# An attention and mixture-of-experts kernel: leftover router weights on VectorE, earlier router steps, and work queued behind the third tile

## Chip, cores and metric

One core of a Trainium2 chip. The metric is device time in microseconds (us) of one execution. The engines are named as in the profile: PE is TensorE, with its weight loads apart as PEld; DVE is VectorE, ACT ScalarE, POOL GpSimd, SP SyncE, which issues most of the transfers.

## What is computed

```python
# q, k, v: (8, 8, 576, 64); causal window of 128, a bias by distance, softmax
attn_out = _attn_ref(**attn_kwargs)
x = attn_out.transpose(0, 2, 1, 3).reshape(B * S, H * D)      # 4608 tokens x 512
logits = x @ w_gate                                           # 8 experts
for idx in np.argsort(-logits.flatten()):                     # best pairs first
    tok, e = idx // E, idx % E
    if assigned[tok] >= 0 or counts[e] >= cap: continue       # cap = 576
    assigned[tok] = e; counts[e] += 1
for e in range(E):
    mask = assigned == e
    out[mask] = np.maximum(x[mask] @ w1[e], 0) @ w2[e]        # 512 -> 1024 -> 512
```

Each expert gets exactly 576 tokens. The assignment is greedy over all token-expert pairs, so the experts fill one after the other.

## The kernel before

**Attention** works on 32 pairs of heads in a software pipeline, with an order written out by hand, and takes the first 204 us or so. It leaves the token rows x in DRAM and the router's scores `L_sb` on the chip.

**The router** (`Router`) finds the experts in the order in which they fill: phase k yields the list of the 576 tokens (`idx[k]`) and the number (`ei[k]`) of the k-th expert to fill. A phase is a chain of small VectorE operations and tiny matmuls on PE that count tokens over 64 thresholds at a time. Phases are Python generators: each `yield` ends a step, and the code that lays out the expert matmuls calls `next(route)` at chosen places, so that the steps lie between matmuls. Phase 0 is `phase0`, driven through `go()` inside `first_expert`; phases 1 to 7 are `phase`. A phase begins with `first_choice` (each token's best expert among the weights that are left: b, ne, cand, am, OH), goes on with `ends`, three counting rounds in `few` (a step ending in an indicator `ind`, a step with the count matmuls and `sat`, and so on), then `totals`, `members`, `positions`, `hits` and `rows`, which writes `idx`. `later` (L908 to L920) then works out the weights left over for the next phase, `L1`; after it come four small operations on a flag that asks for an exact second pass if something did not come out.

**The experts** (`MoE`). The tokens of an expert are gathered by GpSimd in five tiles g of 128 rows (the last of 64), `gather`. `flip` transposes a tile with four PE transposes into the PSUM tile pg (one buffer) and ScalarE copies it rounded into xh; `under` has VectorE write the remainder xl = pg - xh. Weights come in four chunks of 512 KB for each layer (`raw`, four buffers); `split` makes `hl` from each: ScalarE casts the high part (L1041), VectorE subtracts two halves of the low part (L1047, `low`). A layer then takes three matmuls for each product (high x high, low x high, high x low). Layer 1 sums into ph (four buffers), ScalarE applies the relu into hh (L1116), VectorE writes the remainder hlo (L1127). Layer 2 sums into po; its result o is scattered by GpSimd (L1167).

The second expert's layer 1 runs in halves (tokens 0 to 287 first, then the rest), so it can begin when three of its five tiles are turned.

**The order of work.** While `r.nc` and `m.nc` are `OrderedCore`, each engine keeps the order in which the program names its instructions; their records all show L463, the helper's line. After `r.nc = m.nc = nc` the scheduler of the framework orders the instructions by priority (their order in the program) and modelled readiness. GpSimd and SP are never held by `OrderedCore`.

- In `first_expert`, `go(n)` takes n steps of phase 0, `m.low` a weight half on VectorE, `keep_warm(n)` issues n matmuls on zeros (numbers in `ZEROS`).
- Layer 2 of the first expert is laid out with a stop after each of its 40 groups of matmuls (eight for each of five tiles; three matmuls in a group, two in the last tile's). `ROUTE_2`, `ROUTE_3`, `LOAD_2`, `SPLIT_2` and `TURN_2` name the groups behind which a step of the router, a load of a weight chunk of the second expert, a `split` of a chunk, or a flip of one of its tiles is put. What is left of the splits and flips follows behind group 40, with the unordered engines.
- From the second expert on, `slot(k, i)` runs at 31 places i of expert k (0 to 15 in layer 1, 16 to 30 in layer 2). It takes a router step if the waiting count allows and phase k + 1 is not done, or phase k + 2 is not done and i has reached `AHEAD[min(k, 2)]`; it loads and splits by `W_LOAD` and `W_SPLIT`; from i = 16 on it gathers and flips the next expert's tiles.

Of the kernel before, what the change touches and what calls it, by code (L numbers as in the profile page):

```python
# [418 lines left out]

CONST_AT = 4  # L420
WARM, WARM0, WARM1 = 11, 16, 4
AHEAD = 18, 0, 0
ZEROS = 2, 4, 1, 2, 5
CHOICE_1 = 1, 4
HIGHS_2 = 0, 3, 4, 5
LOWS_2 = 0, 0, 0, 2, 1, 2, 2, 1
ROUTE_2 = 11, 12, 14, 15, 17, 18, 19, 22, 26
ROUTE_3, SOONER = (33, 37), (1, 2)
LOAD_2 = {20: 2, 33: 1, 37: 1}
SPLIT_2 = 31, 33  # L430
TURN_2 = 36, 38, 40
W_LOAD = [(0, 1, 0, 0), (0, 1, 1, 2), (0, 1, 2, 6), (0, 1, 3, 10),
          (1, 0, 0, 13), (1, 0, 1, 16), (1, 0, 2, 19), (1, 0, 3, 22), (1, 1, 0, 28)]
W_SPLIT = [(0, 1, 0, 2), (0, 1, 1, 6), (0, 1, 2, 10), (0, 1, 3, 14),
# [36 lines left out]
class Router:  # L471
# [287 lines left out]
    def phase0(self):  # L759

        nc, rt, rs = self.nc, self.p["rt"], self.p["rs"]
        self.pen = self.small("pen", 8)
        nc.vector.memset(self.pen, 0.0)
        nc.vector.tensor_copy(self.left, self.C["e8"])
        b, am, OH = self.b0, self.am0, self.OH0
        lo, w, rw = self.first
        c0, cl = FIRST - 1, self.c0
        self.clamp(cl, b, lo, w, c0)
        key = self.place(cl, lo, rw, c0)
        ind = rt.tile([128, NT, J], BF, name="ind", bufs=1)  # L770
        for a, z in self.halves(c0, NT):
            self.indicate(ind, key, a, z)
        cnt = self.count(ind, OH, c0, NT)
        w2, low = self.small("w"), self.small("low")
        nc.vector.tensor_tensor(low, lo, w, ALU.subtract)
        nc.vector.tensor_scalar(w2, w, 1.0 / J, None, ALU.mult)
        self.place(cl, lo, rw, 0, c0, key)
        rw2 = self.small("rw")
        nc.vector.tensor_scalar(rw2, rw, float(J), None, ALU.mult)
        lo, m, ex, v = self.first_full(cnt, self.part, key, am, w, low)  # L780
        w, rw = w2, rw2
        key = self.place(cl, lo, rw)
        hits = self.ahead_hits(m, ex)
        for s in (1, 2):
            ind = rt.tile([128, NT, J], BF, name="ind", bufs=1)
            for i, (a, z) in enumerate(self.halves(0, NT)):
                if s == 1 and i == 0:
                    self.indicate(ind, key, a, z)
                    self.ahead_rows(hits)
                    yield  # L790
                else:
                    self.indicate(ind, key, a, z)
            low = self.small("low")
            nc.vector.tensor_tensor(low, lo, w, ALU.subtract)
            if s == 1:
                w2, rw2 = self.small("w"), self.small("rw")
                nc.vector.tensor_scalar(w2, w, 1.0 / J, None, ALU.mult)
                nc.vector.tensor_scalar(rw2, rw, float(J), None, ALU.mult)
            yield
            cnt = self.count(ind, OH, 0, NT)  # L800
            yield
            n = self.enough(cnt, self.pen)
            next(n)
            yield
            try:
                next(n)
            except StopIteration as e:
                n = e.value
            yield
            if s == 1:  # L810
                lo2 = self.small("lo")
                nc.vector.scalar_tensor_tensor(lo2, w, n[:, 0:1], low, ALU.mult, ALU.add)
                lo, w, rw = lo2, w2, rw2
                key = self.place(cl, lo, rw)
        sel, rest = (rt.tile([128, NT], BF, name=name, bufs=1) for name in ("sel0", "rsel"))
        nc.vector.tensor_scalar(sel, key[:, :, 0], 1.0, n[:, 0:1], ALU.add, ALU.is_ge)
        nc.vector.tensor_tensor(rest, self.rest, sel, ALU.mult)
        m, ex = self.members(am, v[:, 0:1], rest, NT)
        nc.vector.scalar_tensor_tensor(self.hi, w, n[:, 0:1], low, ALU.mult, ALU.add)
        sp = self.bank()  # L820
        self.positions(sp, m, ex, NT)
        nc.tensor.matmul(sp[:, 64:65], self.C["ones"], self.run[:, NT - 1:NT], start=True, stop=True)
        yield
        hits = self.hits(sp, m, NT, 3, nc.scalar, 2)
        off = self.small("off")
        nc.vector.tensor_scalar(off, sp[:, 64:65], float(CAP - AHEAD_ROWS), None, ALU.not_equal)
        yield
        idx = rs.tile([128, 5], I32, name="idx", bufs=4)
        self.rows(self.bank(), hits, NT, 3, idx)
        self.idx[0] = [self.few_rows[:, t:t + 1] for t in range(2)] + [idx[:, t:t + 1] for t in range(3)]  # L830
        yield
        T1 = rt.tile([128, 8, NT], BF, name="T1")
        nc.vector.tensor_tensor(T1, OH, bc(sel.unsqueeze(1), [128, 8, NT]), ALU.mult)
        nc.vector.tensor_tensor(self.flag, self.flag, off, ALU.max)
        yield
        Dc, keyv, mx = self.totals(T1)
        yield
        nc.vector.tensor_tensor(off, mx, v, ALU.not_equal)
        nc.vector.tensor_tensor(self.flag, self.flag, off, ALU.max)
        self.later(0, self.L0, T1, Dc, keyv, mx)  # L840
        yield

    def halves(self, c0, c1):
# [16 lines left out]
    def phase(self, k, exact=False):  # L860
# [38 lines left out]
        self.later(k, L, T1, Dc, keyv, mx)  # L899
        if k == 1:  # L900
            yield 0

    def later(self, k, L, T1, Dc, keyv, mx):

        nc, rt = self.nc, self.p["rt"]
        if k < 7:
            self.pen = self.small("pen", 8)
            nc.vector.tensor_scalar(self.pen, Dc, float(CAP), -BIG, ALU.is_ge, ALU.mult)  # L908
            self.base = self.small("base", 8)
            nc.vector.tensor_tensor(self.base, self.pen, Dc, ALU.add)  # L910
            nc.vector.scalar_tensor_tensor(self.left, keyv, mx[:, 0:1], self.left, ALU.not_equal, ALU.mult)
            L2 = rt.tile([128, 8, NT], F32, name="L2", bufs=1)
            eng = nc.vector if k == 0 else self.tc.nc.gpsimd
            eng.tensor_tensor(L2, L, bc(self.pen.unsqueeze(2), [128, 8, NT]), ALU.add)
            if k == 0:
                nc.vector.scalar_tensor_tensor(self.L1, T1, 100.0 * BIG, L2, ALU.mult, ALU.add)
            else:
                Lt = rt.tile([128, 8, NT], F32, name="Lt", bufs=1)
                eng.tensor_scalar(Lt, T1, 100.0 * BIG, 1.0, ALU.mult, ALU.mult)
                eng.tensor_tensor(self.L1, Lt, L2, ALU.add)  # L920
        ov = self.small("ov")
        nc.vector.tensor_reduce(ov, Dc, AX.X, ALU.max)
        nc.vector.tensor_scalar(ov, ov, float(CAP), None, ALU.is_gt)
        nc.vector.scalar_tensor_tensor(ov, mx, 0.0, ov, ALU.is_equal, ALU.max)
        nc.vector.tensor_tensor(self.flag, self.flag, ov, ALU.max)
# [98 lines left out]
class MoE:  # L1024
# [61 lines left out]
    def under(self, h, r, ps):  # L1086

        xh, xl = (x[:, :, 128 * h:128 * h + r] for x in self.xg)
        self.nc.vector.tensor_tensor(xl, ps[:, :, :r], xh.bitcast(F32), ALU.subtract)  # L1089

    def turn(self, gs):

        for h, g, r in gs:
            self.under(*self.flip(h, g, r))
            yield

    def hidden(self):

# [119 lines left out]
def first_expert(tc, P, C, r, m, route):  # L1218
# [7 lines left out]
    def go(n=1):  # L1226
        for _ in range(n):
            next(p)
# [24 lines left out]
    m.idle = P["ps_h"].tile([128, 512], F32, name="ph")  # L1253
    W = [m.high(raw[c]) for c in range(2)]
    go(2)
    m.low(W[0], raw[0], 0)
    m.keep_warm(ZEROS[0])
    go(2)
    m.low(W[0], raw[0], 1)
    m.keep_warm(ZEROS[1])  # L1260
    go(2)
    m.low(W[1], raw[1], 0)
    a0 = m.flip(*ga[0], "o")
    m.keep_warm(ZEROS[2])
    go(2)
    a1 = m.flip(*ga[1])
    m.keep_warm(ZEROS[3])
    go()
# [55 lines left out]
            m.low(*lows.pop(0))  # L1324
    rest(7, 1)
    next(route)
    return V


def layer_moe(tc, P, C, r, m, exact):  # L1330
# [12 lines left out]
    def part(e, layer):  # L1343
        W[e, layer].append(m.split(raws[e, layer][len(W[e, layer])]))
# [25 lines left out]
    if exact:  # L1370
        r.start(True)
        W[0, 0] = [m.split(raw) for raw in m.loads(r.ei[0], 0)]
        for _ in m.turn(m.gather(r.idx[0])):
            pass
        for _ in m.layer1(W.pop((0, 0))):
            pass
        V = [m.split(raw) for raw in m.loads(r.ei[0], 1)]
        while 1 not in r.idx:
            next(route)
    else:  # L1380
        V = first_expert(tc, P, C, r, m, route)
    i = 0
    for _ in m.layer2(V, m.h, r.idx[0], fine=True):
        i += 1
        if i in ROUTE_2 and not exact:
            next(route)
        if i == ROUTE_2[-1]:
            r.nc = nc
            gathers[0] = m.turn(m.gather(r.idx[1]))
        if i in ROUTE_3:  # L1390
            next(route)
        for _ in range(LOAD_2.get(i, 0)):
            load(1, 0)
        if i in SPLIT_2:
            part(1, 0)
        if i in TURN_2:
            next(gathers[0])
    r.nc = m.nc = nc
    while len(W[1, 0]) < 4:
        part(1, 0)  # L1400
    for _ in gathers[0]:
        pass
    for k in range(1, E):
        i = 0
        for _ in m.layer1(W.pop((k, 0)), k == 1):
# [95 lines left out]
```

## Time and profile before

| | |
|---|---|
| median of 3 runs | 697.83 us (696.14 to 698.83) |
| the profiled execution: its own time | 698.43 us |
| its span, first to last instruction | 696.7 us |
| mean granted PE clock | 0.979 |
| PE busy | 664.7 us (95%) |
| VectorE busy | 459.6 us (66%) |
| ScalarE busy | 326.7 us (47%) |
| GpSimd busy | 150.5 us (22%) |
| first expert's first matmul | 223.69 us |
| second expert's first matmul | 291.07 us |

A row of a timeline reads: start in us, duration in us, engine, line, operation, out<-in, count, and in brackets the time that the engine stood idle before it and what ended that. A row of sums by stretch reads: stretch, its length, then the busy time and the number of instructions of PE, PEld, VectorE, ScalarE and GpSimd, the mean PE clock, the busy share of the DMA engines and GB/s.

### The profile page before, as it was taken

What the parts mean: (1) busy time and instruction counts of PE and PEld (TensorE: products, weight loads), DVE (VectorE), ACT (ScalarE), POOL (GpSimd) and SP (SyncE); (2) the same over time, 40 slices, a digit from 0 to 9 for tenths busy, and PEclk for the clock granted to TensorE, in tenths of its full rate; (3) what the DMA queues carried; (4) which work ended last, traced back from release to release, by engine and by line L of the source; (5) the groups of instructions that cost most, each with busy time, mean ns of one, the idle gap of its engine ahead of it and who ended that gap; (6) DMA issues with size and microseconds to landing.
All of it is one profiled execution on the core that took longest, in us unless ns stands there. A gap on an engine that the chain in (4) does not pass through costs nothing.

```text
span 696.7 us, 18902 instructions
## 1 busy us (share of the span) xinstructions
PE 664.7 (95%) x7274; PEld 582.6 (84%) x7274; DVE 459.6 (66%) x1903; ACT 326.7 (47%) x992; POOL 150.5 (22%) x337
## 2 busy tenths in 40 slices
PE   8999999999967999799999999999999999999995
PEld 5899899988864987598689789889988988988985
DVE  6778887887878777789698738828847525423310
ACT  6998898988942431523243233224314324322210
POOL 4122222122211103303231231131132022011011
PEclk9999999999995999799999999999999999999999
DMA  8475766667324504604546245145135325201001
GB/s 300 150 229 178 222 196 208 202 205 210 108 70 144 168 16 151 211 1 171 185 119 215 77 135 168 37 129 182 58 109 178 95 92 169 90 30 39 1 24 49
DMA packets 35139, 92.72 MB, mean 133 GB/s; under 512 B 3808, under 2 KB 13152, under 8 KB 35040
## 3 DMA queue, kind: packets, MB, share of 16 engines
q1 hardware_dynamic: 29152, 72.55, 32.4%
q0 software_dynamic: 5888, 18.88, 8.3%
q8 instruction: 59, 0.97, 0.6%
q14 instruction: 40, 0.33, 0.2%
HBM read 72.54 MB, written 18.87 MB: 131 GB/s over the span
## 4 chain that ended last, share of the span: by engine, by line
PE 79%; DVE 11%; ACT 3%; DMA 3%; issue 2%; POOL 1%; SPq 0%; POOLq 0%; ACTq 0%; DVEq 0%
PE ph L1110 21%; PE po L1155 8%; PE po L1156 8%; PE po L1158 6%; PE pt L53 6%; PE x L53 6%; PE s L53 6%; PE pt L160 6%; PE ph L463 4%; DVE hl L1047 2%; PE po L463 2%; DMA raw<-in_w_dram 2%; ACT u L147 2%; PE pg L1082 2%; DVE hlo L1127 1%
## 5 line engine op out<-in xcount | busy, mean ns | idle before, releaser
L1110 PE MATMUL ph<-xh,hl 128*128 128x288 f32 x896 | 168.0, 300 | 1.2 <-ACT xh L463 1.2
L1110 PEld LDWEIGHTS ph<-xh,hl 128*128 128x128 f32 x896 | 136.2, 190 | 2.5 <-ACT xh L463 1.6
L147 ACT ACTIVATE u<-u,mn 128x192 f32<-128x192 f32 (+2 forms) x288 | 124.1, 439 | 5.7 <-DVE mn L137 5.7
L1155 PE MATMUL po<-hl,hh 128*128 128x512 f32 (+1 forms) x288 | 114.3, 397 | 0.0
L1156 PE MATMUL po<-hl,hh 128*128 128x512 f32 (+1 forms) x288 | 110.9, 385 | 0.0
L1110 PE MATMUL ph<-xl,hl 128*128 128x288 f32 x448 | 102.2, 298 | 0.0
L1116 ACT ACTIVATE hh<-ph 128x288 fp32r<-128x288 f32 x112 | 41.0, 409 | 129.9 <-PE ph L1110 127.9
L137 DVE CUSTOM_DVE_ANT_0 u<-s,bm 128x192 f32<-128x192 f32 (+1 forms) x248 | 71.8, 345 | 29.9 <-PE s L53 29.4
L1158 PE MATMUL po<-hl,hlo 128*128 128x512 f32 (+1 forms) x232 | 89.4, 385 | 0.0
L1167 POOL DMA_INDIRECT out_dram<-o,idx x38 | 41.9, 1102 | 189.9 <-ACT o L1162 104.9
L1047 DVE TENSOR_TENSOR hl<-raw,hl 128x512 fp32r<-128x512 f32 x108 | 71.9, 681 | 11.8 <-ACT hl L1041 11.4
L1110 PEld LDWEIGHTS ph<-xl,hl 128*128 128x128 f32 x448 | 74.2, 189 | 0.0
L1089 DVE TENSOR_TENSOR xl<-pg,xh 128x512 fp32r<-128x512 f32 (+1 forms) x32 | 20.2, 632 | 76.7 <-ACT xh L1083 73.3
L1127 DVE SCALAR_TENSOR_TENSOR hlo<-ph,hh 128x288 fp32r<-128x288 f32 (+1 forms) x112 | 43.8, 417 | 38.7 <-ACT hh L1116 37.3
L1041 ACT CAST hl<-raw 128x1024 fp32r<-128x1024 f32 x54 | 55.3, 1050 | 16.5 <-DMA raw<-in_w_dram 12.7
L1155 PEld LDWEIGHTS po<-hl,hh 128*128 128x128 f32 x288 | 54.2, 188 | 9.6
L1156 PEld LDWEIGHTS po<-hl,hh 128*128 128x128 f32 x288 | 54.3, 188 | 9.4
L53 PE MATMUL s<-qk 64*64 64x192 f32 (+1 forms) x992 | 59.9, 325 | 1.1 <-DMA qk<-in_qk_dram 0.8
L147 ACT ACTIVATION_READ_ACCUMULATOR u<-u,mn 128x1 f32 x288 | 56.3, 195 | 0.0
L1162 ACT COPY o<-po 128x512 f32<-128x512 f32 (+1 forms) x29 | 16.6, 572 | 83.6 <-PE po L1158 53.3
L160 PE MATMUL pt<-ident_sb,u 128*128 128x128 f32 x368 | 52.8, 279 | 0.7 <-ACT u L147 0.4
L1063 POOL DMA_INDIRECT g<-x,idx x38 | 39.0, 1025 | 61.4 <-PE pg L1082 30.7
(314 smaller groups left out, 1124.4 us busy)
## 6 DMA issues: line engine op xcount, KB each, us to landing
raw<-in_w_dram SPq DMA_DIRECT2D x64, 512.0 KB, 3.4
qk<-in_qk_dram SPq DMA_DIRECT2D x32, 576.0 KB, 5.4
v<-in_v_dram SPq DMA_DIRECT2D x32, 288.0 KB, 3.6
x<-xb SPq DMA_DIRECT2D x14, 512.0 KB, 4.1
x<-xb SPq DMA_DIRECT2D x8, 128.0 KB, 3.4
x<-xb SPq DMA_DIRECT2D x4, 256.0 KB, 2.3
g<-x,idx POOLq DMA_INDIRECT x38
out_dram<-o,idx POOLq DMA_INDIRECT x38
```

The costliest lines, as they stand in the source:

```text
L53: put(nc.tensor.matmul(out, w, a, start=start, stop=stop, skip_group_check=True))
L137: put(nc.vector.tensor_tensor_reduce(out=weights(n, t, h), in0=x[:, c:c + 64 * m].rearrange("q (j k) -> q j k", k=64), in1=bm[n % NP][:, y ...
L147: put(nc.scalar.activation(u, u, AF.Exp, bias=st["mn"][:, i:i + 1], scale=-1.0, accum_out=st["sm"][:, i:i + 1]))
L160: put(nc.tensor.transpose(ps[:, c:c + 128], u[:, o + 128 * j:o + 128 * j + 128], ident))
L1041: self.nc.scalar.copy(hl[:, 0, :], raw)
L1047: self.nc.vector.tensor_tensor(hl[:, 1, c:c + 512], raw[:, c:c + 512], hl[:, 0, c:c + 512].bitcast(F32), ALU.subtract)
L1110: self.nc.tensor.matmul(pp[t], w[:, a, j, fo:fo + 128], x[:, j, cut[t]:cut[t + 1]], start=(j == 0 and a == 0 and x is xh), stop=(j == 3 an ...
L1127: self.nc.vector.scalar_tensor_tensor(d, pp[t][:, c0:c1], 0.0, o[:, c0:c1].bitcast(F32), ALU.max, ALU.subtract)
L1155: nc.tensor.matmul(out, a, wh, start=(f == 0), stop=False)
L1156: nc.tensor.matmul(out, a, wl, start=False, stop=(f == 7 and t == 4))
L1158: nc.tensor.matmul(out, hl[:, f, 128 * t:128 * t + 128], wh, start=False, stop=(f == 7))
L1167: self.sent = self.tc.nc.gpsimd.indirect_dma_start(out=self.out, out_offset=bass.IndirectOffsetOnAxis(ap=idx[t][:r], axis=0), in_=o[:r, :] ...
```

## The change

- `later` for phase 1 (k = 1) runs on VectorE: its two operations on the full weights replace three on GpSimd. The flag operations are taken out of it into a new method `excess`, called after the `yield 0` that ends phase 1. Phase 0 gets one more step: `later` first, and the flags in a step of their own, which layer 2 of the first expert takes behind group 29 (`FLAG_2`).
- The router steps of phase 1 lie two groups sooner in layer 2, at 9 to 24.
- All four weight chunks of the second expert's layer 1 are loaded behind group 18; two are split behind groups 25 and 27; the third flip comes behind group 39 instead of 40.
- The two first steps of phase 2 (`first_choice` and `ends`), which stood behind groups 33 and 37, the other two splits and the last two flips are put in a block `issue_after(turned.ins)`: on VectorE, what is traced in it is queued behind the xl of the third tile.
- In `first_expert` the weight halves move behind later steps of phase 0, and two matmuls on zeros go.
- `AHEAD` is 24 instead of 0 for the experts from the second on.

```diff
-AHEAD = 18, 0, 0
-ZEROS = 2, 4, 1, 2, 5
+AHEAD = 18, 24, 24
+ZEROS = 1, 3, 1, 2, 5
...
-ROUTE_2 = 11, 12, 14, 15, 17, 18, 19, 22, 26
-ROUTE_3, SOONER = (33, 37), (1, 2)
-LOAD_2 = {20: 2, 33: 1, 37: 1}
-SPLIT_2 = 31, 33
-TURN_2 = 36, 38, 40
+ROUTE_2 = 9, 10, 12, 13, 15, 16, 17, 20, 24
+SOONER = 1, 2
+LOAD_2 = {18: 4}
+SPLIT_2 = 25, 27
+FLAG_2 = 29
+TURN_2 = 36, 38, 39
...
         Dc, keyv, mx = self.totals(T1)
         yield
+        self.later(0, self.L0, T1, Dc, keyv, mx)
+        yield
+        nc.vector.tensor_tensor(self.flag, self.flag, off, ALU.max)
         nc.vector.tensor_tensor(off, mx, v, ALU.not_equal)
         nc.vector.tensor_tensor(self.flag, self.flag, off, ALU.max)
-        self.later(0, self.L0, T1, Dc, keyv, mx)
+        self.excess(Dc, mx)
         yield
...
         self.later(k, L, T1, Dc, keyv, mx)
         if k == 1:
             yield 0
+        self.excess(Dc, mx)
...
-            eng = nc.vector if k == 0 else self.tc.nc.gpsimd
+            eng = nc.vector if k < 2 else self.tc.nc.gpsimd
             eng.tensor_tensor(L2, L, bc(self.pen.unsqueeze(2), [128, 8, NT]), ALU.add)
-            if k == 0:
+            if k < 2:
                 nc.vector.scalar_tensor_tensor(self.L1, T1, 100.0 * BIG, L2, ALU.mult, ALU.add)
...
     go(2)
-    m.low(W[0], raw[0], 0)
     m.keep_warm(ZEROS[0])
     go(2)
+    m.low(W[0], raw[0], 0)
+    m.keep_warm(ZEROS[1])
+    go()
     m.low(W[0], raw[0], 1)
-    m.keep_warm(ZEROS[1])
-    go(2)
-    m.low(W[1], raw[1], 0)
+    go()
     a0 = m.flip(*ga[0], "o")
     m.keep_warm(ZEROS[2])
     go(2)
+    m.low(W[1], raw[1], 0)
     a1 = m.flip(*ga[1])
...
         if i == ROUTE_2[-1]:
-            r.nc = nc
             gathers[0] = m.turn(m.gather(r.idx[1]))
-        if i in ROUTE_3:
-            next(route)
+        if i == FLAG_2 and not exact:
+            next(p)
...
         if i in TURN_2:
-            next(gathers[0])
+            turned = next(gathers[0])
     r.nc = m.nc = nc
-    while len(W[1, 0]) < 4:
-        part(1, 0)
-    for _ in gathers[0]:
-        pass
+    with tc.issue_after(turned.ins):
+        for _ in range(2):
+            next(route)
+        while len(W[1, 0]) < 4:
+            part(1, 0)
+        for _ in gathers[0]:
+            pass
```

More of the change, by code (lines that the diff above doesn't have):

```diff
@@ L833, in phase0 @@
         nc.vector.tensor_tensor(T1, OH, bc(sel.unsqueeze(1), [128, 8, NT]), ALU.mult)
-        nc.vector.tensor_tensor(self.flag, self.flag, off, ALU.max)
         yield
@@ L920, in later, with excess @@
                 eng.tensor_tensor(self.L1, Lt, L2, ALU.add)
+    def excess(self, Dc, mx):
+        nc = self.nc
         ov = self.small("ov")
@@ L1088, in under @@
         xh, xl = (x[:, :, 128 * h:128 * h + r] for x in self.xg)
-        self.nc.vector.tensor_tensor(xl, ps[:, :, :r], xh.bitcast(F32), ALU.subtract)
+        return self.nc.vector.tensor_tensor(xl, ps[:, :, :r], xh.bitcast(F32), ALU.subtract)
     def turn(self, gs):
         for h, g, r in gs:
-            self.under(*self.flip(h, g, r))
-            yield
+            yield self.under(*self.flip(h, g, r))
     def hidden(self):
@@ L1326, in first_expert @@
     next(route)
-    return V
+    return V, p
 def layer_moe(tc, P, C, r, m, exact):
@@ L1380, in layer_moe @@
     else:
-        V = first_expert(tc, P, C, r, m, route)
+        V, p = first_expert(tc, P, C, r, m, route)
     i = 0
```

## Prediction

> **What bounds the kernel now.** I read the page's engine table first, then sums by stage, then the timelines of the stage with the worst sum.
>
> ```profile
> PE 664.7 (95%) x7274; PEld 582.6 (84%) x7274; DVE 459.6 (66%) x1903; ACT 326.7 (47%) x992; POOL 150.5 (22%) x337
> ```
>
> TensorE (PE) is the bound over the whole span, so time can come only from stretches in which PE stands or runs slowly. The sums by stretch (PE, weight load, VectorE, ScalarE, GpSimd busy, then PE's clock) show where:
>
> ```profile
> 278.20:291.10 12.90, 8.25 (x33) 5.48 (x31) 9.61 (x20) 7.18 (x9) 6.62 (x7) 0.75 0.79 258
> 291.10:321.50 30.40, 29.22 (x218) 27.73 (x219) 25.26 (x105) 8.62 (x18) 2.66 (x4) 0.94 0.13 46
> 321.50:356.70 35.20, 33.53 (x197) 25.77 (x196) 28.19 (x115) 13.58 (x19) 11.79 (x12) 1.00 0.50 169
> 415.70:472.80 57.10, 56.98 (x376) 50.27 (x375) 37.80 (x136) 18.30 (x34) 12.89 (x13) 1.00 0.37 115
> ```
>
> The last row is a later expert: PE 56.98 of 57.10, nothing to gain. The first row is the end of the first expert, where its last tile, the next tiles' transposes and the next router phase meet: PE works 8.25 of 12.90 us, at a mean clock of 0.75. Rows two and three are the second expert's two layers; VectorE works 25.26 of 30.40 there, 83%. PE's timeline of the first stretch:
>
> ```profile
> 280.57 0.66 PE L463 MATMUL pg<-ident_sb,g 128*128 128x128 f32 x4 [0.36 <-DMA g<-x,idx]
> 280.99 0.70 PE L463 MATMUL po<-hl,hh 128*128 128x512 f32 x2
> 281.73 0.27 PE L529 MATMUL m<-ident_sb,ext 128*1 128x128 f32 x1
> 281.75 0.70 PE L463 MATMUL po<-hl,hh 128*128 128x512 f32 x2
> 285.46 1.11 PE L463 MATMUL pg<-ident_sb,g 128*128 128x128 f32 x4 [3.01 <-DVE xl L463]
> 286.23 2.06 PE L463 MATMUL po<-hl,hh 128*128 128x512 f32 x4
> 288.22 0.58 PE L536 MATMUL m<-ed,craw 1*128 1x1 f32 x2
> 288.73 1.12 PE L463 MATMUL pg<-ident_sb,g 128*128 128x128 f32 x4
> 291.07 0.61 PE L1110 MATMUL ph<-xh,hl 128*128 128x288 f32 x1 [1.23 <-ACT xh L463]
> ```
>
> Three flips (pg, four transposes each) must precede the second expert's first matmul (ph, 291.07). There is one pg buffer, so the second flip waits 3.01 us for VectorE's xl of the first. VectorE was then doing this:
>
> ```profile
> 280.31 0.68 DVE L510 TENSOR_REDUCE b<-L 128x36 f32<-128x288 f32 x1 [1.71 <-POOL L L920]
> 281.02 0.46 DVE L512 TENSOR_TENSOR ne<-L,b 128x288 bf16<-128x288 f32 x1
> 281.40 0.18 DVE L524 TENSOR_REDUCE ext<-b 128x1 f32<-128x36 f32 x1
> 281.51 0.46 DVE L514 SCALAR_TENSOR_TENSOR cand<-ne,c_eb 128x288 bf16<-128x288 bf16 x1
> 282.00 0.66 DVE L516 TENSOR_REDUCE am<-cand 128x36 bf16<-128x288 bf16 x1
> 282.70 0.31 DVE L517 TENSOR_TENSOR OH<-c_eb,am 128x288 bf16<-128x288 bf16 x1
> 282.92 1.28 DVE L463 TENSOR_TENSOR hl<-raw,hl 128x512 fp32r<-128x512 f32 x2
> 284.13 0.68 DVE L1047 TENSOR_TENSOR hl<-raw,hl 128x512 fp32r<-128x512 f32 x1
> 284.73 0.68 DVE L463 TENSOR_TENSOR xl<-pg,xh 128x512 fp32r<-128x512 f32 x1
> ```
>
> The next phase's first choice (b to OH) sat 1.71 us at the head of VectorE's queue until GpSimd had written the leftover weights; xl stood behind it and behind three weight halves (hl). On GpSimd those leftovers lie between the gathers:
>
> ```profile
> 275.94 1.00 POOL L1063 DMA_INDIRECT g<-x,idx  x1 [1.50 <-issue]
> 276.93 1.11 POOL L914 TENSOR_TENSOR L<-L,pen 128x288 f32<-128x288 f32 x1
> 278.19 1.25 POOL L1063 DMA_INDIRECT g<-x,idx  x1 [0.15 <-issue]
> 279.46 0.82 POOL L920 TENSOR_TENSOR L<-Lt,L 128x288 f32<-128x288 f32 x1
> ```
>
> The third flip's xh lost time in the same way, on ScalarE, behind a weight cast that waited for a late load:
>
> ```profile
> 289.49 1.04 ACT L1041 CAST hl<-raw 128x1024 fp32r<-128x1024 f32 x1 [2.29 <-DMA raw<-in_w_dram]
> 290.44 0.58 ACT L463 CAST xh<-pg 128x512 fp32r<-128x512 f32 x1
> ```
>
> **The change part by part.**
>
> *1. The flips at the end of the first expert.* Three things leave xl's and xh's way: the first choice and two of four weight chunks go behind the third tile's xl; the leftovers move to VectorE, two groups earlier; the four loads go out together at group 18 instead of 20, 33 and 37, so no cast waits 2.29 us. The gathers come sooner by two groups, and the second one also by the 1.11 us of L914 that stood before it, the later ones by the 0.82 us of L920 too; so the first flip's 0.36 us wait goes. PE was free for that flip at 280.57 - 0.36 = 280.21 and began layer 1 at 291.07: 10.86 us. After the change the limit is the round trip through the one pg buffer: flip 0.66 + xh 0.58 + xl 0.68 + about 0.2 of hand-overs (estimate) = 2.1 us from flip to flip. Four matmuls at half clock took 2.06, so a group of two takes some 0.5 us at full; two groups lie in the first round trip and one in the second, and neither fills 2.1. The third flip gives 2.0 more until layer 1 has xh and xl. 2.1 + 2.1 + 2.0 = 6.2, against 10.86: **4.7 us**. What is late next is that round trip: PE then waits some 0.4 and 0.9 us before the flips. Bounds: 2.5, if ScalarE still puts the two moved casts (1.04 each) between the flips; 5.6, if PE only waits behind the last flip.
>
> *2. The clock of the second expert's start.* PE's clock in the two half-microseconds where it changes:
>
> ```profile
> 284.50:285.00 0.50, 0.00 (x0) 0.00 (x0) 0.50 (x2) 0.22 (x1) 0.30 (x1) 0.57 0.19 74
> 294.50:295.00 0.50, 0.50 (x4) 0.50 (x4) 0.50 (x3) 0.33 (x1) 0.00 (x0) 0.69 0.00 0
> ```
>
> A mean of 0.57 puts the fall to 0.5 at 284.57, and 0.69 the rise to 1.0 at 294.81. Layer 1 began at 291.07, so 3.74 us of it ran at half speed and did 1.87 us of work. With waits of 0.9 us and less, PE has no stretch like the 3.01 us one; I take the clock to stay up: **1.9 us**. Bounds 0 and 1.9. [...] The trace agrees only in part: the fall came while the 3.01 us gap was still open, some 2 us into it, so an accumulation of shorter waits isn't excluded by it (second rival).
>
> *3. What is put behind the third tile comes back.* VectorE then owes layer 1 of the second expert the first choice (0.68 + 0.46 + 0.18 + 0.46 + 0.66 + 0.31 = 2.75) and four weight halves (0.68 each, 2.7): 5.5 us that partly ran in PE's idle time. That layer had 30.40 - 25.26 = 5.14 us free on VectorE, and loses 1.9 of length; the room is about used up. PE's queue holds router matmuls that wait for VectorE, and half of the weights is wanted midway in the layer. I take **2.0 us lost**; bounds 0 (all fits between) and 5.5 (all of it on the path).
>
> *4. The third router phase leaves the second expert* (AHEAD 24: its steps run only late in layer 2 and go on in the expert behind). In layer 2 one such step cost PE:
>
> ```profile
> 340.32 0.42 PE L600 MATMUL m<-OHf,ind 128*128 128x16 bf16 x8 [1.67 <-DVE ind L576]
> ```
>
> That goes, less a little that appears one expert on: **1.5 us**; bounds 0 and 1.7. In the experts behind, as many steps run as before, only elsewhere: 0, with bounds of 1.5 either way (a few tenths in each of five experts).
>
> *5. The start of the first expert.* VectorE's first weight half now follows the router's count instead of leading it:
>
> ```profile
> 214.71 0.69 DVE L463 TENSOR_TENSOR hl<-raw,hl 128x512 fp32r<-128x512 f32 x1 [0.72 <-ACT hl L463]
> 215.44 0.17 DVE L463 TENSOR_TENSOR odd<-m,pen 64x8 f32<-64x8 f32 x1
> ```
>
> The count's odd could start about 0.95 us sooner (0.72 of waiting, most of the 0.69). The chain then meets the warming matmuls on zeros ahead of the first real one:
>
> ```profile
> 222.51 1.53 PE L463 MATMUL ph<-zero 128*128 128x512 bf16 x5
> 223.69 0.47 PE L463 MATMUL ph<-xh,hl 128*128 128x256 f32 x1
> ```
>
> Those five stay, and at half clock they are no shorter; two earlier ones go. I take **0.5 us** won; bounds -1.5 (the clock rises later with fewer zeros) and 0.95.
>
> *6. Small ones, at nothing.* The leftovers on VectorE cost two operations like
>
> ```profile
> 239.17 0.45 DVE L463 TENSOR_TENSOR L<-L_sb,pen 128x288 f32<-128x288 f32 x1
> ```
>
> so 0.9 us, ahead of the weight halves of groups 25 and 27. Cover: the indices were ready before the first gather's 275.94 and come two groups sooner (a group of three matmuls takes some 0.7 us), near 274.5; with the leftovers 0.9, four halves 2.7 and six small flag operations of some 0.18 like ext, VectorE is through near 279.2, and the first xl is wanted only when flip and xh are done, after 281. Without that cover each microsecond would delay xl by one. The router steps two groups sooner want their first indicator two groups sooner:
>
> ```profile
> 257.74 0.69 DVE L463 TENSOR_TENSOR ind<-kf,c_i 128x1024 bf16<-128x1024 bf16 x1
> ...
> 258.54 0.62 PE L463 MATMUL po<-hl,hh 128*128 128x512 f32 x2
> ```
>
> It ends at 258.43, and the tenth group of layer 2 began at 258.54: just in time for a step after the ninth, 0 to 0.2 lost, and the distances between the steps stay as they are. The loads pass nothing on SP's queue; in the DMA engines they stand ahead of the gathers (third rival).
>
> **The sum.** 4.7 + 1.9 - 2.0 + 1.5 + 0.5 = 6.6 us, off the profiled execution's 698.43: 691.8. That execution lies 0.6 above the median of the runs shown, 697.83, so I forecast **691.2 us**.
>
> **The rivals.** *First: VectorE becomes the second expert's bound.* All 5.5 us of part 3 lands on the path, in waits like the 1.67 us one and in casts and halves that come late; the gain is then 4.7 + 1.9 - 5.5 + 1.5 + 0.5 = 3.1, which gives 698.43 - 3.1 - 0.6 = 694.7. For it: the 83%. Against: xl, hl and hlo already fill each other's gaps there.
>
> *Second: the clock falls all the same.* The waits of part 1 fall close together, PE would work about half of some three microseconds, and the trace has a fall about 2 us into a gap. Part 2's 1.9 goes: 691.2 + 1.9 = 693.1. With some of the first rival beside it, it ends near 695.
>
> *Third: it doesn't do what it says, since the tiles come late.* Four loads of 512 KB now go ahead of the gathers; at the 258 GB/s of the first stretch they take 8.1 us. If the gathers wait behind them and the first tile comes 4 us later than 280.57, part 1 shrinks to about 1 and the clock falls: 4.7 - 3.7 + 0 - 2.0 + 1.5 + 0.5 = 1.0, 696.8. Against: the loads start about ten microseconds before the first flip.
>
> *Fourth, slower: the late router.* With AHEAD 24, phase k + 2 ends in the middle of layer 1 of expert k + 1, just ahead of the slots that load and gather by it. Each of the five experts behind could get waits of 1.67 us on PE where before nothing waited. From two such waits in each (16.7 us) it ends at 691.2 + 16.7 = 708; it outweighs the gain from 1.3 us per expert. Against: VectorE has 57.10 - 37.80 = 19.3 us free in such an expert.
>
> **How the numbers follow.** Forecast 0.55, first rival 0.15, second 0.12, third 0.08, fourth 0.10. The forecast's own range is 688 to 694.5 by the bounds of parts 1, 3 and 5. The range to hold 8 in 10 goes up through the first three rivals and leaves out the fourth and the best corner: 687.5 to 698.5. A measurement tells about 0.5% (3.5 us) from no change, so faster is below 694.3: the forecast but for its upper end (0.50), and most of the second rival and part of the first (0.13): 0.63. Slower by as much is the fourth rival, 0.09; the rest, 0.28, is no change.
>
> **What would show it.** Part 1: from the first flip to the first ph some 6 us instead of 10.5, xl right behind xh, no L914 or L920 on GpSimd between the gathers, no cast waiting for DMA. Part 2: clock 1.00 throughout. Part 3: first-layer length of the second expert, 30.5 before, 28 to 31 after; VectorE busy there near 90%. Part 4: no 1.67 us wait in its second layer. Part 5: first ph of the first expert 0.5 sooner. The forecast is wrong if flips still wait 3 us, if the clock falls again, or if PE's idle time appears in the experts behind.

## The result: slower by about 4 us, and the profile after

| | before | after |
|---|---|---|
| median of 5 runs each | 697.67 us | 702.09 us (700.11 to 703.26) |
| ratio, 95% interval | | 1.0063 [1.0040, 1.0085] |
| profiled execution, its own time | 698.43 us | 700.11 us |
| its span and mean clock | 696.65 us, 0.979 | 698.24 us, 0.979 |

The forecast was 691.2 us, with a range up to 698.5. The profiled execution of the changed kernel is the lowest of its five, 2.0 under their median, so its stages show less of the loss than the runs have.

Line numbers in the changed kernel lie up to eight higher: its helper's line is L464, its gather's L1071. The sums by stretch of the changed kernel, for the stretches that answer to those of before (end of the first expert; layer 1 and layer 2 of the second; a later expert):

```profile
276.50:289.13 12.63, 8.04 (x33) 5.71 (x31) 5.17 (x15) 5.67 (x9) 3.93 (x4) 0.77 0.81 281
289.13:321.03 31.90, 30.90 (x237) 28.91 (x237) 28.03 (x115) 9.29 (x20) 2.88 (x4) 0.98 0.02 6
321.03:356.39 35.36, 31.01 (x161) 24.30 (x162) 23.49 (x73) 12.96 (x17) 9.61 (x9) 0.95 0.52 183
414.21:472.03 57.82, 57.03 (x376) 50.14 (x375) 38.31 (x136) 18.66 (x33) 12.63 (x13) 1.00 0.32 114
```

The first row is hardly better than before: PE 8.04 of 12.63 us at a clock of 0.77, though VectorE now works only 5.17 us there. The third row is new: PE stands for 4.35 of 35.36 us, where it stood for 1.67 of 35.20. PE's timeline at both places:

```profile
279.25 0.60 PE L464 MATMUL pg<-ident_sb,g 128*128 128x128 f32 x4
...
284.82 1.12 PE L464 MATMUL pg<-ident_sb,g 128*128 128x128 f32 x4 [4.04 <-DVE xl L464]
...
287.34 1.12 PE L464 MATMUL pg<-ident_sb,g 128*128 128x128 f32 x4 [0.55 <-DVE xl L464]
...
289.13 1.30 PE L1117 MATMUL ph<-xh,hl 128*128 128x288 f32 x4
...
334.38 0.93 PE L1090 MATMUL pg<-ident_sb,g 128*128 128x128 f32 x4 [4.35 <-DMA g<-x,idx]
```

The first flip no longer waits for its tile. The second waits longer than before, 4.04 instead of 3.01 us, and again for xl; the second expert's first flip of a tile for the third expert waits 4.35 us for a gather, where it did not wait at all. ScalarE and VectorE at the first place:

```profile
281.79 1.04 ACT L1049 CAST hl<-raw 128x1024 fp32r<-128x1024 f32 x1 [3.00 <-DMA raw<-in_w_dram]
282.74 0.58 ACT L464 CAST xh<-pg 128x512 fp32r<-128x512 f32 x1
283.95 1.05 ACT L1049 CAST hl<-raw 128x1024 fp32r<-128x1024 f32 x1 [0.62 <-DMA raw<-in_w_dram]
```

```profile
282.87 1.29 DVE L1055 TENSOR_TENSOR hl<-raw,hl 128x512 fp32r<-128x512 f32 x2 [4.92 <-ACT hl L1049]
284.08 0.68 DVE L464 TENSOR_TENSOR xl<-pg,xh 128x512 fp32r<-128x512 f32 x1
...
290.52 0.66 DVE L511 TENSOR_REDUCE b<-L 128x36 f32<-128x288 f32 x1
```

At the head of ScalarE's queue stood a weight cast whose load had not landed, for 3.00 us; xh came behind it. VectorE, idle for 4.92 us, then took that chunk's two halves before xl. By the order in the program these are the first two chunks of the second expert's **layer 2**. They are split in `slot`, after the block that queues things behind the third tile, and no longer in the fixed order, so the scheduler could put them in front. The last row is the start of router phase 2: 290.52, against 280.31 before. Its ids were ready at 327.24 (324.68 before), and GpSimd issued the first gather 0.8 us later, as it did before:

```profile
328.02 1.49 POOL L1071 DMA_INDIRECT g<-x,idx  x1 [7.90 <-issue]
```

The same gather and its flip before the change (GpSimd's timeline, then PE's):

```profile
325.45 1.05 POOL L1063 DMA_INDIRECT g<-x,idx  x1 [7.29 <-PE ph L1110]
```

```profile
331.87 0.60 PE L1082 MATMUL pg<-ident_sb,g 128*128 128x128 f32 x4
```

After the change PE reached the flip at 330.03, 1.8 us sooner than before, and the gather was issued 2.6 us later, so that the tile came only at 334.38.

### The profile page after: what moved, and what is told of

Its sections match the earlier page's. It is cut to its first block, busy times and chain, and to the rows that moved or that the text cites. A ratio compares the mean times of both kernels' runs of the same rounds, so it can differ in the third digit from the quotient of the medians.

```text
span 698.2 us, 18881 instructions
## 1 busy us (share of the span) xinstructions
PE 663.4 (95%) x7271; PEld 581.9 (83%) x7272; DVE 462.3 (66%) x1905; ACT 328.3 (47%) x992; POOL 148.1 (21%) x334
## 4 chain that ended last, share of the span: by engine, by line
PE 84%; DVE 7%; ACT 3%; issue 3%; DMA 2%; POOL 0%; POOLq 0%; DVEq 0%; ACTq 0%; SPq 0%
PE ph L1117 23%; PE po L1162 9%; PE po L1163 9%; PE po L1165 7%; PE x L53 6%; PE pt L53 6%; PE s L53 6%; PE pt L160 6%; PE ph L464 4%; PE pg L1090 2%; PE po L464 2%; ACT u L147 2%; DMA g<-x,idx 1%; DMA raw<-in_w_dram 1%; PE x L1446 1%
## 5 line engine op out<-in xcount | busy, mean ns | idle before, releaser
L1174 POOL DMA_INDIRECT out_dram<-o,idx x38 | 40.4, 1063 | 208.8 <-ACT o L1169 101.0
L1055 DVE TENSOR_TENSOR hl<-raw,hl 128x512 fp32r<-128x512 f32 x108 | 69.9, 684 | 11.7 <-ACT hl L1049 10.8
L1071 POOL DMA_INDIRECT g<-x,idx x38 | 40.8, 1073 | 69.9 <-issue 50.5
L1165 PEld LDWEIGHTS po<-hl,hlo 128*128 128x128 f32 x232 | 43.9, 189 | 9.0
```

What stands on the lines that cost most here:

```text
L1055: self.nc.vector.tensor_tensor(hl[:, 1, c:c + 512], raw[:, c:c + 512], hl[:, 0, c:c + 512].bitcast(F32), ALU.subtract)
L1165: nc.tensor.matmul(out, hl[:, f, 128 * t:128 * t + 128], wh, start=False, stop=(f == 7))
```

## Experiments

The table gives, from PE's timelines, the time from the first expert's first matmul on ph to the second expert's (A), the second expert (B), the other six to the start of the last matmul (C), and their sum, in us; two times are counted from the same first matmul: the phase's first row (b<-L) and its ids for the third expert. The stretch before that matmul is left out: 222.96 to 225.24 us among these profiled executions. "Ratio" is to the runs of before in the same comparison. Each row of times is one execution. The expectations below count experts from 0: their experts 2 to 7 are the third to the eighth.

| kernel | A | B | C | sum | phase 2 starts | ids | ratio |
|---|---|---|---|---|---|---|---|
| before | 67.38 | 65.65 | 332.38 | 465.41 | 56.62 | 100.99 | |
| after | 66.17 | 67.26 | 335.60 | 469.03 | 67.56 | 104.28 | 1.0063 |
| e1_hold | 62.16 | 68.90 | 335.47 | 466.53 | 63.54 | 103.50 | 1.0033 |
| e2_ahead0 | 66.43 | 68.95 | 333.85 | 469.23 | | | 1.0056 |
| e3_fliplate | 66.48 | 62.33 | 335.71 | 464.52 | 67.86 | 104.95 | 0.9999 |
| e5_ahead24 | 67.25 | 61.73 | 335.17 | 464.14 | | | 0.9982 |
| e6_both | 62.96 | 67.41 | 335.70 | 466.07 | 64.35 | 104.87 | 1.0001 |
| e7_apart | 62.49 | 66.38 | 336.96 | 465.83 | | | 1.0021 |
| e8_both_ahead0 | 61.68 | 68.87 | 334.71 | 465.26 | | | 1.0017 |
| e4_first | 66.62 | 65.56 | 332.18 | 464.35 | | | 0.9999 |
| e9_route_back | 66.99 | 62.95 | 335.50 | 465.44 | 53.86 | 99.87 | 0.9969 |
| e10_hold_route | 62.19 | 62.26 | 335.62 | 460.07 | 54.19 | 97.35 | 0.9950 |
| e11_hold_route0 | 63.35 | 63.97 | 333.21 | 460.53 | | | 0.9939 |
| e12_hold_route_24_0 | 63.04 | 62.15 | 334.92 | 460.11 | | | 0.9929 |

### The casts in front of the tiles: e1_hold

The changed kernel, with the splits of the second expert's first two layer-2 chunks queued behind the third tile's xh and xl:

```diff
-        W[e, layer].append(m.split(raws[e, layer][len(W[e, layer])]))
+        with ExitStack() as es:
+            if (e, layer) == (1, 1) and len(W[1, 1]) < 2:
+                for at in behind:
+                    es.enter_context(tc.issue_after(at.ins))
+            W[e, layer].append(m.split(raws[e, layer][len(W[e, layer])]))
...
+            behind = [turned, m.rounded]
```

> The changed kernel, with the first two casts and the four halves of the second expert's layer-2 weights queued on ScalarE and VectorE behind the third tile's xh and xl. Theory 1 (heads of queues): the first stretch was not shortened because a cast of the NEXT layer's weights stood ahead of xh and waited 3.00 us for its load; then the time from first flip to first ph goes from 9.9 us to 6.2 to 7, xh follows its flip at once, and the kernel is 2.5 to 4 us faster than the changed one (about 698 to 699.5). Rival (the one pg buffer and the half clock are the limit): 9 us and more remain and the time stays at 701 to 703.

Measured: 699.36 us, ratio 1.0033 [1.0019, 1.0047]. PE's timeline:

```profile
279.87 0.60 PE L464 MATMUL pg<-ident_sb,g 128*128 128x128 f32 x4
...
281.97 0.63 PE L464 MATMUL pg<-ident_sb,g 128*128 128x128 f32 x4 [0.57 <-DMA g<-x,idx]
...
284.00 0.66 PE L464 MATMUL pg<-ident_sb,g 128*128 128x128 f32 x4 [0.93 <-DVE xl L464]
...
285.33 0.79 PE L1117 MATMUL ph<-xh,hl 128*128 128x288 f32 x4 [0.22 <-ACT xh L464]
...
334.84 1.12 PE L1090 MATMUL pg<-ident_sb,g 128*128 128x128 f32 x4 [5.24 <-DMA g<-x,idx]
```

From first flip to layer 1 it is 5.47 us instead of 9.88, and the clock stays up there (1.00 from 275.20 to 299.09): A falls by 4.0 us, so those casts and halves were the cause at the first place. But B gives 1.6 of these back: the wait for the gather grew from 4.35 to 5.24, and the stretch at half clock around it is 6.83 us long (333.22 to 340.05) instead of 3.42. The phase began 4.0 us sooner (63.54) and its ids came only 0.8 sooner (103.50). Measured from layer 1's first matmul it began no sooner at all: 1.4 us behind it in both kernels. That VectorE is nearly full in that layer (28.03 of 31.90 us in the changed kernel) may be why its end hardly follows; no run shows it.

### The late gather: e3_fliplate

The changed kernel, with the first flip in the second expert three slots later: `i + TURN_WAIT + 3 * (k == 1)`.

> The changed kernel with the flips of the third expert's tiles three slots later in the second expert. Theory 3: PE stood 4.35 us in the second expert's layer 2 before a flip, since the gather began 2.6 us later than before while the flip stood 2.0 us earlier in PE's queue; with the flip some 5 us later that wait falls under 1 us, the half-clock stretch at 334.6 goes too (1.7 us), and the kernel is 4 to 6 us faster than the changed one (696 to 698). Rival (the tiles are late for the third expert in any case): the wait comes back at the end of that layer 2, gain under 1.5 us.

Measured: 697.13 us, 0.9999 [0.9986, 1.0012]. B falls by 4.9 us; the wait at the flip is nearly gone:

```profile
335.18 0.66 PE L1090 MATMUL pg<-ident_sb,g 128*128 128x128 f32 x4 [0.34 <-DMA g<-x,idx]
```

So the wait of 4.35 us and the half clock behind it were worth about 5 us in these two executions. The gather itself came no sooner; PE was given other matmuls meanwhile.

### Where the third phase starts: e2_ahead0 and e5_ahead24

The changed kernel with `AHEAD = 18, 0, 0`, and the kernel before with `AHEAD = 18, 24, 24`.

> The changed kernel with AHEAD back at 18, 0, 0, so that phase 3 is again routed in the second expert. Theory 2 (a phase moved is a phase paid elsewhere, and 0.6 us more in each expert): experts 2 to 7 go back from 335.6 to about 332.4 us, the second expert becomes 2.5 to 4.5 us longer than its 67.3, total within 1.5 us of the changed kernel. Rival (the late router saves what the prediction said): the second expert becomes longer by 1.5 and the others do not change, total 1.5 us above the changed kernel. Rival 2 (AHEAD alone makes the change slow): total at or below the kernel before, 697.7 or less.

> The kernel before with AHEAD 18, 24, 24 alone. Theory 2: its second expert (65.65 us) is 2 to 5 us shorter without phase 3, experts 2 to 7 some 3.2 us longer, total within 1.5 us of before. As predicted (rival): 1.5 us faster, with the later experts unchanged. The prediction's fourth rival: waits in every later expert, 5 us slower or more.

Measured: 701.29 us, 1.0056 [1.0037, 1.0075]; and 696.57 us, 0.9982 [0.9966, 0.9998]. In the changed kernel the late start is worth 1.7 us in B and costs 1.8 in C. In the kernel before it is worth 3.9 in B and costs 2.8 in C. It mostly moves a cost from the second expert into the six behind it, and part of that cost is work: in C, VectorE has 610 instructions and 184.8 us in the changed kernel, 565 and 175.7 before, since most of phase 3 now runs there (its ids come 25.6 us into the third expert, 5.6 before). PE works 1.3 us more in C and stands 3.2 us instead of 1.2. What the standing looks like, in the changed kernel's third expert (PE's timeline, then VectorE's):

```profile
374.69 0.19 PE L712 MATMUL m<-ex,c_ones 128*128 128x36 bf16 x1 [0.80 <-DVE ex L705]
```

```profile
373.90 0.64 DVE L511 TENSOR_REDUCE b<-L 128x36 f32<-128x288 f32 x1
374.47 0.16 DVE L705 TENSOR_TENSOR ex<-run,m 128x36 bf16<-128x36 bf16 x1
```

VectorE does the next phase's first row before the row for which PE stands. Experts three to six each have one such wait of 0.8 us, in the changed kernel and in e5_ahead24; the kernel before has none above 0.4 there. (The expectations of e7_apart and e12_hold_route_24_0 put these waits at 0.96 us; the traces show 0.8.)

### Both repairs, and two variants: e6_both, e7_apart, e8_both_ahead0

e6_both joins e1's hold and e3's late flip; e7_apart adds a stop at the end of every phase (`if k: yield 0`); e8_both_ahead0 has `AHEAD = 18, 0, 0` on e6_both.

> The changed kernel with both repairs: the next layer's casts and halves held behind the third tile, and the third expert's flips three slots later in the second expert. Theories 1 and 3 together: the 4.5 us of the first stretch (flip to ph 5.5 instead of 9.9) and the 5 us of the second (no wait over 1 us, no half clock there) add up, since nothing links them: 693 to 694.5, ratio to before 0.993 to 0.996. Rival (one eats the other): the second expert's gather is still late and the time is 696 to 697.5, no better than the later flips alone.

> As the one with both repairs, and every phase ends in a step of its own, so that the next phase's first choice no longer lies in the queue of the phase before (until now so for phase 1 alone). Theory 4: the 0.96 us that PE stands in each of experts 2 to 5 before positions comes from the first choice's reduction that VectorE does ahead of ex; it goes, and experts 2 to 5 are 0.5 to 0.9 us shorter each: 2 to 3.5 us faster than with the two repairs. Rival (the wait is the length of the chain itself): within 0.8 us of it.

> As the one with both repairs, with AHEAD back at 18, 0, 0. Theory 2: phase 3 returns to the second expert, which gets 3 to 4.5 us longer, and experts 2 to 7 get 3 us shorter: within 1.5 us of the kernel with both repairs, most likely slower by 1. The prediction's part 4: slower by 1.5 with the later experts unchanged. Rival (AHEAD costs three microseconds net): faster by 2 or more.

Measured: 698.32 us, 1.0001 [0.9982, 1.0019]; 699.0 us, 1.0021 [1.0002, 1.0039]; 697.9 us, 1.0017 [0.9996, 1.0038]. The repairs did not add up: e6_both came out above its theory and its rival. Its ids came at 104.87, as late as in e3, while PE was 3.5 us further on:

```profile
336.97 0.66 PE L1090 MATMUL pg<-ident_sb,g 128*128 128x128 f32 x4 [3.68 <-DMA g<-x,idx]
```

What was won at the start of the second expert was lost in its second layer: against e3, 3.3 us more of waiting and 1.7 in a stretch of half clock behind it (338.11 to 341.52). Neither repair took phase 2 from behind the third tile; the hold had brought its first row 3.5 us sooner than in e3 (64.35 for 67.86), but not its ids. e7's stops changed nothing: its experts three to six still wait 0.8 us for the positions, and C is longer by 1.3. e8_both_ahead0 lies within 0.4 us of e6_both, as its theory had it.

### The first expert's new order alone: e4_first

The kernel before with the moved weight halves and `ZEROS = 1, 3, 1, 2, 5`.

> The kernel before with the change of first_expert's start alone (weight halves behind later steps, two matmuls on zeros fewer). The prediction's part 5: the first ph of the first expert 0.5 us sooner, the whole within 0.7 us of before, the clock's rise no later relative to the first ph. Rival (fewer zeros keep the clock low longer): first layer of the first expert 1 us longer or more, whole slower by 0.5 to 1.5 us.

Measured: 697.37 us, 0.9999 [0.9981, 1.0017]; its first matmul on ph is at 223.66, against 223.69. No effect that can be measured.

### Phase 2 back to its old place: e9_route_back and e10_hold_route

The phase's first two steps are taken out of the block behind the third tile; e10 has e1's hold as well:

```diff
+        if i in (33, 37):
+            r.nc = nc
+            next(route)
...
     with tc.issue_after(turned.ins):
-        for _ in range(2):
-            next(route)
         while len(W[1, 0]) < 4:
```

> The changed kernel with one part undone: the first two steps of the second expert's router phase are issued from groups 33 and 37 of the first expert's second layer again, not behind its third tile; everything else (weights behind the third tile, sooner steps, the later phase's start) stays. Theory (the wait of the second expert's flip on its gathered tile, 4.35 us, comes from this phase starting at 290.5 instead of 280.3 us): its first choice runs at about 281 to 284 us on VectorE, the ids for the third gather are ready 3 to 5 us sooner, the wait before that flip falls below 1 us, no stretch of half clock follows it: 4 to 5 us less than the changed kernel, 697 to 698.5. Rival (VectorE is the limit there, so the steps put ahead of the tiles' subtractions only move the wait to the start of the second expert): its first layer starts up to 2.6 us later and the time is 700 to 702.

> The same, and the casts and halves of the second expert's first two layer-2 chunks are queued behind the third tile's cast and subtraction as in the first experiment. Theory (two separate faults, one wait at each end of the second expert, both from what the change put behind the third tile): 5.5 us from first flip to first layer at the start and no wait over 1 us for the gathered tile later: 693 to 695. Rival (VectorE or the phase itself sets the gathered tile's time, as in the run that joined the hold with the later flip, where the time saved at the start came back as a wait of 3.8 us for the gathered tile): 697 to 698.5.

Measured: e9 696.75 us, 0.9969 [0.9954, 0.9985]; e10 694.25 us, 0.9950 [0.9929, 0.9972]. In e9 the gather and the flip (GpSimd's timeline, then PE's):

```profile
323.64 1.07 POOL L1071 DMA_INDIRECT g<-x,idx  x1 [7.30 <-issue]
```

```profile
284.82 1.11 PE L464 MATMUL pg<-ident_sb,g 128*128 128x128 f32 x4 [3.89 <-DVE xl L464]
...
330.36 0.60 PE L1090 MATMUL pg<-ident_sb,g 128*128 128x128 f32 x4
```

The gather is issued 4.4 us sooner than in the changed kernel and the flip waits for nothing; B is 62.95. The wait at the first place stays (3.89). In e10 both places are better:

```profile
279.57 0.60 PE L464 MATMUL pg<-ident_sb,g 128*128 128x128 f32 x4
...
281.84 0.63 PE L464 MATMUL pg<-ident_sb,g 128*128 128x128 f32 x4 [0.55 <-issue]
...
284.14 0.63 PE L464 MATMUL pg<-ident_sb,g 128*128 128x128 f32 x4 [0.90 <-DVE lo L541]
...
285.45 0.79 PE L1117 MATMUL ph<-xh,hl 128*128 128x288 f32 x4 [0.21 <-ACT xh L464]
...
325.94 0.66 PE L1090 MATMUL pg<-ident_sb,g 128*128 128x128 f32 x4 [1.28 <-DMA g<-x,idx]
```

(The row `lo` that ends the wait of 0.90 us is a router row that VectorE queues right behind the second tile's xl.) It is 5.88 us from first flip to layer 1, with the first choice on VectorE before it:

```profile
277.44 0.66 DVE L511 TENSOR_REDUCE b<-L 128x36 f32<-128x288 f32 x1
```

A wait of 1.28 us for the gather is left, where the theory had none over 1. From its issue to the flip this gather took 4.56 us (from 321.38, DMA engines 57% busy), against 6.36 in the changed kernel (73%) and 7.39 in e1_hold (92%); so the gathers' own length is a part of these waits too, which no run tried apart.

Against the changed kernel's ratio of 1.0063, the hold alone takes 0.30%, the phase alone 0.94%, both together 1.13%, each known to about 0.3% by the intervals. That is what two separate faults would give; the share of the phase is clear of the noise, that of the hold alone barely, and the traces carry it (A falls by 4.0 us in e1, by 4.8 from e9 to e10). The first choice in front of the tiles costs nothing that shows in A (62.19 with it, 62.16 without). What the early start gives the phase: its first indicator comes 13.9 us behind layer 1's first matmul in e10 (13.5 before the change), 17.7 in the changed kernel and 19.8 in e1.

### The versions with both repairs: e11_hold_route0 and e12_hold_route_24_0

e10 with `AHEAD = 18, 0, 0`, and with `18, 24, 0`.

> The same as the one before with the third phase begun in the second expert from group 0 again (18, 0, 0 instead of 18, 24, 24). Theory (moving that phase only moves its cost between the second expert and the five behind it): within 1 us of the one before, 693 to 695.5. Rival (without the third phase the second expert has room on VectorE that the repaired order needs): 1.5 to 3 us slower than the one before.

> The run with hold and router steps put back, with only the later experts' phases begun from group 0 again (18, 24, 0); the second expert keeps the changed kernel's start at group 24. Theory (the 0.96 us wait of the matmul for the positions in each of the four experts from the third to the sixth is VectorE doing the next phase's first choice ahead of the row that is waited for, because a late start makes the two fall together): those four waits go or shrink, the second expert keeps its 62.3 us, the experts behind take 1.5 to 3 us less: 691.5 to 693. Rival (each phase costs its expert about the same wherever it starts, so the cost only changes its place): 693.5 to 694.5, as with 18, 24, 24.

Measured: 693.06 us, 0.9939 [0.9915, 0.9963]; 693.54 us, 0.9929 [0.9904, 0.9953]. Sums of 460.53 and 460.11 beside e10's 460.07: where the later phases start makes no difference that these runs can tell. In e12 two of the four waits for the positions stayed (0.80 and 1.05 us), one of 1.10 us for ed came in their place, and C fell by only 0.7: its theory failed and its rival held. All three are faster than both kernels, by 0.5 to 0.7% than before; they cannot be told apart from one another.

## Why the prediction was wrong, by its own steps

**Part 1, the flips (4.7 us): failed.** From the first flip to layer 1 it took 9.88 us, not 6.2: 1.0 gained. The step took the queues of ScalarE and VectorE to hold only what the change names. It had the right danger as its lower bound, casts between the flips, but for the wrong chunks: the moved ones stayed behind the third tile, and the next layer's first two took their place, at 1.04 us each on ScalarE and 1.29 on VectorE, and 3.00 us of waiting for a load on top. So even the bound of 2.5 was too high. With these held (e1, e10), 5.47 and 5.88 us stand beside the predicted 6.2. The round trip through one pg buffer was sized rightly: in e8_both_ahead0, where both later flips wait for xl, it is 2.00 and 2.09 us from flip to flip, with waits of 0.47 and 0.97, and in e1 2.03 from the second to the third (281.97 to 284.00), with a wait of 0.93 for xl; the 2.0 behind the third flip were 1.3 (284.00 to 285.33 in e1). It is not always the limit: in e6_both and e7_apart these flips wait 0.76 to 1.53 us for their gathers, a small case of the third rival.

**Part 2, the clock (1.9): half right.** It fell again (second rival), but layer 1 spent only 1.12 us at half rate (to 290.25) instead of 3.74: about 1.3 gained. The forecast took the absence of a wait near 3 us to be enough; that was the author's assumption, and no run shows it. Of the kernels with the hold, e1, e7 and e10 kept the clock at 1.00 there; in e6, whose waits there are 0.97 and 1.45 us, it fell to 0.50 for 3.41 us, and for as long in e11 (from 285.50) and e12 (from 285.99).

**Part 3 (2.0 lost): the size of what it named was near, and it missed the main effect.** Layer 1 of the second expert grew from 30.47 to 31.90 us though 1.3 us of half-rate time went: 2.7 lost. But the part counted the moved steps as work, not as the head of a chain with a due time. Phase 2 began 10.2 us later, its ids came 2.6 later while PE came to the flip that needs them 1.8 sooner: together about the 4.35 us of waiting. With 3.42 us at half clock, 1.7 of that lost, it makes 6.1 us; e3 and e9, which take the wait away in two ways, give 0.64% and 0.94% back. This step decided the sign: e9, which undoes it alone, is faster than the kernel before (0.9969).

**Part 4 (1.5 gained, 0 behind): failed in the second half.** The wait of 1.67 us went, but the six experts behind took 335.60 instead of 332.38 us, 3.2 lost, past the bound of 1.5. The step had as many router steps in them as before; they have most of phase 3 more, 9.1 us of work on VectorE. e5 shows that the late start alone makes C 2.8 us longer, with the four waits of 0.8 us. In the changed kernel e2 takes back 1.8 of the 3.2; where the other 1.5 come from stays open. The waits are the slower rival's mechanism, in four experts and not five, at 0.8 us each, under the 1.3 per expert from which it would decide alone. Why VectorE takes the first choice ahead of ex was not settled: neither e7's stops nor e12's start took the cost away.

**Part 5 (0.5): not shown.** The profile has 0.73, but e4, which does this part alone, is even with before, and the first matmul's time differs by more from one profiled execution to another.

**Part 6: right.** Nothing on the leftover weights stands between the gathers, the first flip has no wait, and from the first expert's first matmul to PE's being free for that flip it took 56.29 us, 56.52 before.

In the profiled executions the terms are: start 0.7 gained, A 1.2 gained, B 1.6 lost, C 3.2 lost: 2.9 lost, of which 1.3 came back after the last matmul, for 1.6 of span; the runs have 4.4. Of the rivals the second came true, and the fourth in small; the wait that cost most stood in none. The time landed outside the range because the late gather behind part 3 and the waits and work behind part 4 were put at nothing, and most of part 1's gain did not come.

## What to carry to other kernels

When a chain of small steps is put behind something to clear a queue, follow the chain to its end: ask when its last result is due, and move the consumer in its queue with it, or leave the chain's head where it was. When work is taken off an engine's queue in a section that a scheduler orders, ask what it will pull in instead; what must not come first has to be tied down too. If two repairs don't add up, look for the result that neither makes earlier.

## What the runs showed of the clock

In the profiles of the two kernels the clock was 1.00 or 0.50, and each stretch of low clock ahead of the last matmul lasted 3.41 us or a multiple of it: 17.07 us in both before the first expert (206.06 to 223.13 before the change, 204.91 to 221.98 after it), then 10.24 before (284.57 to 294.81) and 6.83 and 3.42 after (283.42 to 290.25, 334.62 to 338.04). The stretches at full clock between them were multiples too: 61.44 us in both, and 44.37 after. Counted in stretches of 3.41 us from such an edge, the sums show this (PE busy first, clock third from the end). The changed kernel:

```profile
280.01:283.42 3.41, 0.77 (x4) 0.28 (x2) 0.55 (x1) 1.53 (x2) 1.11 (x2) 1.00 0.97 360
283.42:286.84 3.42, 1.97 (x6) 1.25 (x6) 2.88 (x6) 1.63 (x2) 0.00 (x0) 0.50 0.55 210
286.84:290.25 3.41, 2.91 (x10) 2.37 (x11) 1.55 (x3) 1.53 (x2) 0.00 (x0) 0.50 0.50 159
331.21:334.62 3.41, 0.24 (x2) 0.24 (x3) 0.37 (x1) 0.00 (x0) 2.51 (x3) 1.00 0.88 269
334.62:338.04 3.42, 3.42 (x11) 2.81 (x10) 1.82 (x3) 1.53 (x2) 1.30 (x2) 0.50 1.00 357
```

The two stretches in which PE worked 0.77 and 0.24 us at full clock were each followed by one at 0.50, and the second time PE worked throughout in that one: the wait before 334.38 was over when the clock fell at 334.62, and 3.42 us of full work ran at half rate. e6_both and e10:

```profile
283.50:286.91 3.41, 1.56 (x11) 1.19 (x12) 0.69 (x1) 0.59 (x1) 0.00 (x0) 1.00 0.71 262
286.91:290.32 3.41, 3.41 (x15) 2.86 (x14) 2.51 (x5) 2.81 (x4) 0.00 (x0) 0.50 0.01 4
```

```profile
281.32:284.73 3.41, 1.99 (x13) 1.60 (x14) 1.89 (x8) 0.59 (x1) 0.74 (x1) 1.00 0.81 299
284.73:288.15 3.42, 3.21 (x23) 2.62 (x22) 3.29 (x10) 2.97 (x4) 0.00 (x0) 1.00 0.02 7
```

In e6_both the waits there are 0.97 and 1.45 us, and the clock fell after a stretch with 1.56 us of work; in e10 the stretch had 1.99 and it did not. Counted in the same way, the profiles show at other places: from full clock it fell after 0.00 us of PE work (e1, e3, e7), 0.13 and 1.25 (before), 0.19 (e9), 1.02 (the changed kernel), 1.14 (e6), 1.46 (e11) and 1.92 (e12); it stayed up after 1.83 (e7), 1.88 (the changed kernel, 20.58 to 24.00) and 2.01 (e6). From half it rose after 2.91 (the changed kernel) and 2.96 (e12), and stayed low after 2.79 (e9) and 3.16 (before, 216.31 to 219.72). So these rows give no single figure for either. The stretches begin elsewhere in each execution, at 281.32 in e10, 282.29 in e7_apart and 283.50 in e6_both: e7_apart, with waits of 0.76 and 1.53 us at the same place as e6_both's, had 1.83 us of work in its stretch and kept the clock. So nearly the same waits cost 1.7 us (half of 3.41) in one and nothing in another.
